# First-chunk head of an attention-plus-feed-forward kernel: v in two halves around W, first h block in halves, first q norms from column sums

## The chip, the cores and the metric

The kernel runs on one core of a Trainium2 chip. The metric is device time in microseconds (us) of one execution; lower is better. Most executions agree within 0.3%.

## The reference

```python
qn = q / (np.linalg.norm(q, axis=1, keepdims=True) + 1e-06)    # q, k, v: 4 x 6144 x 256
kn = k / (np.linalg.norm(k, axis=1, keepdims=True) + 1e-06)
s = kn.transpose(0, 2, 1) @ qn / tau                           # 256 x 256 per batch
a = softmax(s)
x = v @ a
h = np.maximum(np.maximum(x @ w1, x @ w2), x @ w3)             # W: 256 x 768
out = h @ w_out                                                # 768 x 256
```

The kernel folds the softmax matrix into W (called `aw`), so that each chunk of 512 tokens needs `v @ aw`, two maxima and the product with W_out.

## The kernel before

The loads are queued by GpSimd in this order: k and q of the first batch, v's first chunk, W in three column parts of three matrices each, v's second chunk. The DMA queue is the limit of this stretch: its share in the prediction's table of windows is 0.96 up to 21 us and 1.11 up to 34.3 (packets of one engine overlap, so a share can pass 1).

```python
    load_v(0)
    for fp in range(d_ff // FT):
        load_w(fp)                     # three loads each: w1, w2, w3
    load_v(1)
    ...
    ps = gram(0)                       # k squares, then q-by-k and q-by-q products (for q's norms)
    warm_ps = htile("warm_ps")
    for i in range(6):
        PE.matmul(warm_ps, lhsT=ident, rhs=warm, start=(i == 0), stop=(i == 5))
    et = softmax_t(*ps)                # VectorE reduces q-by-q diagonals, then Ln, Exp, Exp
    v_transpose_pe(0)
    aw = alloc_aw()
    rinv = aw_first(et, aw)
    v_transpose(1)                     # DMA transpose of v's second chunk, waits for its load
    ...
    hold_loads(1)                      # GpSimd copies one column of that transpose
    POOL.dma_start(out=wo_sb, in_=moe_w_out.rearrange("(fc p) d -> p fc d", p=P))   # W_out
    load_v(2)
    load_v(3)
```

W_out is issued only after `hold_loads(1)`, a copy that waits until v's second chunk has been loaded and transposed. The first output product comes after eight h blocks (all six of the first chunk and two of the second) and the two later parts of `aw`, and it waits for W_out.

## Time and profile before

| | before |
|---|---|
| median of the runs | 573.48 us (573.35 to 573.7) |
| span of the profiled run | 571.9 us |
| v's second chunk issued / landed | 36.74 / 42.38 us |
| W_out landed, first output product starts | 51.02, 51.07 us |

The profile is read from the end of the head backwards: TensorE has no gap from 51.1 to 560 us, so the question is only when it gets there, and the chain of waits names what it was waiting for. The lines are in the prediction below. One view is not in it: GpSimd's own timeline, here of the kernel before (start, duration, instruction, count, and in brackets the idle time ahead of it with what ended it).

```profile
31.94 2.91 POOL L135 DMA_DIRECT2D w_sb<-in_moe_w_dram  x4 [1.38 <-DMA q_sb<-in_q_dram]
35.34 1.41 POOL L135 DMA_DIRECT2D w_sb<-in_moe_w_dram  x2 [0.49 <-DMA v_sb<-in_v_dram]
36.74 0.59 POOL L110 DMA_DIRECT2D v_sb<-in_v_dram  x1
```

Each issue waits for an earlier load to land; the issue at 35.34 waited for v's first chunk, which landed at 35.06, eight loads earlier in the queue.

### The profile page before, as it was taken

To read this page: it belongs to the slowest core of one execution; us is meant where nothing else is said; L and a number is where in the kernel's file an instruction comes from. 1 tells how busy PE (TensorE), PEld (TensorE's weight loads), DVE (VectorE), ACT (ScalarE), POOL (GpSimd) and SP (SyncE) were. 2 spreads that over 40 slices of the span, in tenths; PEclk is the share of its full clock that TensorE was granted. 3 is DMA by queue.
4 is the path that set the end of the run, shared out by engine and by line. 5 is a ranking of instruction groups with operands and counts; after the bars stand their busy time and mean duration, and the time that the engine had idled before them with its cause. 6 is when DMAs were issued, how large, how long until landed. Compare 5 with 4: busy or idle time off the path is not lost.

```text
span 571.9 us, 9438 instructions
## 1 busy us (share of the span) xinstructions
PE 552.9 (97%) x3344; PEld 329.1 (58%) x3344; DVE 415.9 (73%) x658; ACT 309.1 (54%) x540; POOL 233.3 (41%) x237
## 2 busy tenths in 40 slices
PE   3799999999999999999999999999999999999997
PEld 2665555555755555555575555555575555555566
DVE  0048777777887777777767777777768778778775
ACT  1044567767464576776535467767635444444443
POOL 2442357776460078776560048777750000000000
PEclk9999999999999999999999999999999999999999
DMA  9997999895479268975279339985437333132112
GB/s 143 106 147 121 132 238 138 158 133 107 111 83 171 70 109 157 135 149 107 57 133 149 97 79 141 147 143 99 122 81 160 75 77 108 56 104 64 56 55 76
DMA packets 76960, 65.64 MB, mean 115 GB/s; under 512 B 52464, under 2 KB 62576, under 8 KB 76784
## 3 DMA queue, kind: packets, MB, share of 16 engines
q0 software_dynamic: 19072, 26.48, 39.1%
q1 hardware_dynamic: 57696, 38.41, 24.1%
q8 instruction: 26, 0.43, 0.3%
q14 instruction: 22, 0.18, 0.1%
q10 hardware_dynamic: 144, 0.13, 0.1%
HBM read 78.64 MB, written 25.17 MB: 182 GB/s over the span
## 4 chain that ended last, share of the span: by engine, by line
PE 90%; DMA 6%; issue 2%; POOL 1%; DVE 0%; POOLq 0%
PE h_ps L378 64%; PE o_ps L398 22%; DMA v_sb<-in_v_dram 3%; PE gram L249 3%; PE ew_ps L300 2%; DMA q_sb<-in_q_dram 1%; DMA wo_sb<-in_moe_w_out_dram 1%; DMA vt_sb<-v_sb 1%; POOL k_sb L99 0%; PE o_ps L423 0%; POOL w_sb L135 0%; POOL q_sb L102 0%; DVE o_sb L450 0%; POOL ident masks.py:199 0%; PE rs_ps L288 0%
## 5 line engine op out<-in xcount | busy, mean ns | idle before, releaser
L378 PE MATMUL h_ps<-vt_sb,aw_sb 128*128 128x512 bf16 (+1 forms) x1764 | 406.6, 375 | 0.1
L378 PEld LDWEIGHTS <-aw_sb 128*128 128x128 bf16 x1764 | 171.7, 98 | 161.7 <-DVE aw_sb L306 2.4
L383 DVE TENSOR_TENSOR s_mx<-h_ps,s_mx 128x512 bf16<-128x512 f32 (+1 forms) x294 | 198.8, 676 | 82.2 <-ACT s_mx L382 82.0
L382 ACT ACTIVATE s_mx<-h_ps 128x512 bf16<-128x512 f32 (+1 forms) x294 | 172.3, 586 | 124.3 <-PE h_ps L378 123.4
L384 DVE TENSOR_TENSOR ht_sb<-h_ps,s_mx 128x512 bf16<-128x512 f32 (+1 forms) x294 | 200.2, 681 | 30.6
L208 POOL TENSOR_TENSOR acc<-acc,sq 128x768 f32<-128x768 f32 x88 | 144.3, 1649 | 69.3 <-ACT sq L200 53.1
L398 PE MATMUL o_ps<-wo_sb,ht_sb 128*128 128x256 bf16 x1128 | 153.8, 273 | 0.1
L398 PEld LDWEIGHTS <-ht_sb 128*128 128x128 bf16 x1128 | 110.4, 98 | 52.2 <-issue 0.3
L401 ACT ACTIVATE o_sb<-o_ps 128x512 f32<-128x512 f32 x94 | 56.1, 597 | 83.9 <-PE o_ps L398 83.9
L110 POOL DMA_DIRECT2D v_sb<-in_v_dram x48 | 27.8, 584 | 37.4 <-DMA vt_sb<-v_sb 35.2
L200 ACT ACTIVATE sq<-q_sb 128x768 bf16<-128x768 fp8e4 x48 | 40.5, 844 | 0.0
L200 ACT ACTIVATE sq<-k_sb 128x768 bf16<-128x768 fp8e4 x48 | 40.1, 835 | 0.0
L205 POOL CAST acc<-sq 128x768 f32<-128x768 bf16 x6 | 4.9, 821 | 65.7 <-ACT sq L200 65.7
L102 POOL DMA_DIRECT2D q_sb<-in_q_dram x33 | 18.4, 565 | 4.1 <-DMA v_sb<-in_v_dram 3.1
L168 PE MATMUL kk<-k_sb 128*128 128x256 fp8e4 x48 | 7.5, 338 | 12.3 <-DVE k_sb L154 6.5
L99 POOL DMA_DIRECT2D k_sb<-in_k_dram x29 | 16.1, 557 | 2.9 <-issue 1.1
L249 PE MATMUL gram<-k_sb,q_sb 128*128 128x512 fp8e4 x144 | 16.8, 276 | 0.0
L249 PEld LDWEIGHTS <-q_sb 128*128 128x256 fp8e4 x144 | 15.9, 136 | 0.6
L303 ACT ACTIVATE aw_sb<-ew_ps,rinv 128x384 bf16<-128x384 f32 (+1 forms) x24 | 13.1, 554 | 5.7 <-PE ew_ps L300 4.8
L221 POOL PARTITION_ALL_REDUCE tot<-acc x6 | 10.9, 1858 | 11.9 <-DVE s_mx L383 6.0
L300 PE MATMUL ew_ps<-w_sb,et 128*128 128x384 bf16 (+1 forms) x96 | 15.6, 313 | 0.0
L168 PEld LDWEIGHTS <-k_sb 128*128 128x256 fp8e4 x48 | 6.4, 182 | 13.2 <-DMA k_sb<-in_k_dram 6.7
(64 smaller groups left out, 116.5 us busy)
## 6 DMA issues: line engine op xcount, KB each, us to landing
out_dram<-o_sb SPq DMA_DIRECT2D x41, 512.0 KB, 2.9
v_sb<-in_v_dram POOLq DMA_DIRECT2D x48, 256.0 KB, 4.4
k_sb<-in_k_dram POOLq DMA_DIRECT2D x24, 192.0 KB, 5.9
q_sb<-in_q_dram POOLq DMA_DIRECT2D x24, 192.0 KB, 7.3
out_dram<-o_sb SPq DMA_DIRECT2D x13, 256.0 KB, 2.0
k_sb<-in_k_dram POOLq DMA_DIRECT2D x5, 256.0 KB, 11.2
w_sb<-in_moe_w_dram POOLq DMA_DIRECT2D x9, 128.0 KB, 5.7
kf<-in_k_dram SPq DMA_DIRECT2D x1, 1024.0 KB, 5.0
```

Source lines behind the costliest of these rows:

```text
L102: POOL.dma_start(out=qk[b][0][:, g0:g0 + w, :], in_=q_r[b][:, g0:g0 + w, :])
L110: POOL.dma_start(out=t, in_=v_r[gi // NCH, gi % NCH])
L200: ACT.activation(out=sq, in_=src, func=AF.Square)
L208: POOL.tensor_tensor(out=acc, in0=acc, in1=sq, op=ALU.add)
L249: PE.matmul(g[:, j * C:(j + 1) * C], lhsT=qt[:, tsl, j * P:(j + 1) * P], rhs=kt[:, tsl, :], start=(tp == 0 and j == 0), stop=(tp == NG // ...
L300: PE.matmul(ew[:, :w], lhsT=et[:, j, ic * P:(ic + 1) * P], rhs=w_sb[m][:, j, fsl], start=(j == 0), stop=(j == CC - 1))
L378: PE.matmul(t.rearrange("p (t n) -> p t n", n=P), lhsT=aw[m][:, ic, fsl], rhs=vt[:, tsl, ic, :], start=(ic == 0), stop=(ic == CC - 1))
L382: ACT.activation(out=s_mx, in_=hp[0], func=AF.Copy)
L383: DVE.tensor_tensor(out=s_mx, in0=hp[1], in1=s_mx, op=ALU.max)
L384: DVE.tensor_tensor(out=ht, in0=hp[2], in1=s_mx, op=ALU.max)
L398: PE.matmul(st["ps"][:, half], lhsT=ht[:, fc, t * P:(t + 1) * P], rhs=wo_sb[:, fc, :], start=(fc == 0), stop=(fc == FC - 1))
L401: ACT.activation(out=st["o"][:, t - 1:t + 1, :].rearrange("p t d -> p (t d)"), in_=st["ps"], func=AF.Copy)
```

## The change

Its intent is to start the first h block sooner: q's norms are ready earlier (squares on ScalarE and VectorE while q arrives, summed by one-column products, instead of q-by-q products that VectorE reduces at the end); half of v is loaded and transposed while W's first part comes in; and the first h block is cut in two halves of tokens, so that it can start on the first.

```diff
-    load_v(0)
-    for fp in range(d_ff // FT):
+    POOL.dma_start(out=v_tiles[0][:, 0:HT, :], in_=v_r[0, 0][:, 0:HT, :])
+    load_w(0)
+    POOL.dma_start(out=v_tiles[0][:, HT:TPC, :], in_=v_r[0, 0][:, HT:TPC, :])
+    for fp in range(1, d_ff // FT):
         load_w(fp)
...
-                PE.matmul(ps[j][:, C:C + P], lhsT=qt[:, tsl, jsl], rhs=qt[:, tsl, jsl],
-                          start=False, stop=last, perf_mode=DR, skip_group_check=True)
+        def squares(g0, w):
+            ...
+            ACT.activation(out=a[:, 0:h, :], in_=ra, func=AF.Square)
+            DVE.tensor_tensor(out=d[:, 0:h, :], in0=rd, in1=rd, op=ALU.mult)
+        def columns(rows, first=False, last=False):
+            for n, (t, r) in enumerate(rows):
+                for j in range(CC):
+                    PE.matmul(nq[:, j:j + 1], lhsT=t[:, r, j * P:(j + 1) * P], rhs=ones_c, ...)
...
-    for i in range(6):
-        PE.matmul(warm_ps, lhsT=ident, rhs=warm, start=(i == 0), stop=(i == 5))
-    et = softmax_t(*ps)
-    v_transpose_pe(0)
+    for i in range(2):
+        PE.matmul(warm_ps, lhsT=ident, rhs=warm, start=(i == 0), stop=(i == 1))
+    et = softmax_first(*first)
+    v_transpose_pe(0, 0, HT)
     aw = alloc_aw()
     rinv = aw_first(et, aw)
+    v_transpose_pe(0, HT, TPC)
     v_transpose(1)
...
-                h_block(gi, aw, fc)
+                if gi == 0 and fc == 0:
+                    h_block(gi, aw, fc, slice(0, HT))
+                    h_block(gi, aw, fc, slice(HT, TPC))
+                else:
+                    h_block(gi, aw, fc)
```

The order of products inside `aw_first` changes a little as well, and VectorE alone now copies the transposed v out of PSUM (ScalarE had done half). The guard copy and the load of W_out behind it stay as they were.

More of the change, by code (lines that the diff above doesn't have):

```diff
@@ L75 @@
     sq_pool = ctx.enter_context(tc.tile_pool(name="sq", bufs=4))
+    sqq_pool = ctx.enter_context(tc.tile_pool(name="sqq", bufs=3))
     sm = ctx.enter_context(tc.tile_pool(name="sm", bufs=2))
@@ L118 @@
     SP.dma_start(out=kf, in_=k_r[0][:, 0:HEAD, :])
-    for load, widths in ((load_k, [8] * 5), (load_q, [8] * 4 + [4, 4, 4, 2, 2])):
+    QW = [8] * 4 + [4, 4, 4, 2, 2]
+    for load, widths in ((load_k, [8] * 5), (load_q, QW)):
         g0 = HEAD if load is load_k else 0
@@ L135, in load_w @@
             POOL.dma_start(out=wt[:, :, fsl], in_=w.rearrange("(cc p) f -> p cc f", p=P)[:, :, fsl])
-    load_v(0)
-    for fp in range(d_ff // FT):
+    HT = TPC // 2
+    v_tiles[0] = v_pool.tile([P, TPC, C], BF16, name="v_sb")
+    POOL.dma_start(out=v_tiles[0][:, 0:HT, :], in_=v_r[0, 0][:, 0:HT, :])
+    load_w(0)
+    POOL.dma_start(out=v_tiles[0][:, HT:TPC, :], in_=v_r[0, 0][:, HT:TPC, :])
+    for fp in range(1, d_ff // FT):
         load_w(fp)
@@ L157, with gram_first @@
     neg_ln_tau = -math.log(float(tau)) if float(tau) != 1.0 else 0.0
-    def gram(b):
-        qt, kt = qk[b]
+    def gram_first():
+        qt, kt = qk[0]
         kk = htile("kk")
@@ L173, in gram @@
             DVE.tensor_tensor(out=dkm[:, jsl], in0=kk[:, jsl], in1=ident, op=ALU.mult)
-        ps = [xtile(f"gram{j}") for j in range(CC)]
-        for tp in range(NG // 2):
-            tsl = slice(2 * tp, 2 * tp + 2)
-            last = tp == NG // 2 - 1
-            for j in range(CC):
-                jsl = slice(j * P, (j + 1) * P)
-                PE.matmul(ps[j][:, 0:C], lhsT=qt[:, tsl, jsl], rhs=kt[:, tsl, :],
-                          start=(tp == 0), stop=last, perf_mode=DR, skip_group_check=True)
-                PE.matmul(ps[j][:, C:C + P], lhsT=qt[:, tsl, jsl], rhs=qt[:, tsl, jsl],
-                          start=False, stop=last, perf_mode=DR, skip_group_check=True)
-            if tp == 11:
+        g = xtile("gram")
+        nq = htile("nq")
+        def squares(g0, w):
+            h = w // 2
+            a = sqq_pool.tile([P, QW[0] // 2, C], BF16, name="sqa")
+            d = sqq_pool.tile([P, QW[0] // 2, C], BF16, name="sqd")
+            ra, rd = qt[:, g0:g0 + h, :], qt[:, g0 + h:g0 + w, :]
+            ACT.activation(out=a[:, 0:h, :], in_=ra, func=AF.Square)
+            DVE.tensor_tensor(out=d[:, 0:h, :], in0=rd, in1=rd, op=ALU.mult)
+            return [(t, r) for t in (a, d) for r in range(h)]
+        def columns(rows, first=False, last=False):
+            for n, (t, r) in enumerate(rows):
+                for j in range(CC):
+                    PE.matmul(nq[:, j:j + 1], lhsT=t[:, r, j * P:(j + 1) * P], rhs=ones_c,
+                              start=(first and n == 0 and j == 0), stop=(last and n == len(rows) - 1),
+                              skip_group_check=True)
+        g0 = 0
+        rows = None
+        for i, w in enumerate(QW):
+            if rows:
+                columns(rows, first=(i == 1))
+            for tp in range(g0 // 2, (g0 + w) // 2):
+                tsl = slice(2 * tp, 2 * tp + 2)
+                for j in range(CC):
+                    PE.matmul(g[:, j * C:(j + 1) * C], lhsT=qt[:, tsl, j * P:(j + 1) * P], rhs=kt[:, tsl, :],
+                              start=(tp == 0 and j == 0), stop=(tp == NG // 2 - 1), perf_mode=DR,
+                              skip_group_check=True)
+            rows = squares(g0, w)
+            g0 += w
+            if i == 2:
                 kb_ps = htile("kb_ps")
@@ L190, in gram @@
                 ACT.activation(out=rkb, in_=lnk, func=AF.Exp, scale=-0.5)
-        return ps, rkb
+        columns(rows, last=True)
+        return [g[:, j * C:(j + 1) * C] for j in range(CC)], rkb, nq[:, 0:CC]
     SQW = 3
@@ L265, in exp_t, with softmax_first @@
         return et
-    def softmax_t(ps, rkb):
-        n2q = sm.tile([P, CC], FP32, name="n2q")
-        scr = sm.tile([P, P], FP32, name="scr")
-        for j in range(CC):
-            DVE.tensor_tensor_reduce(out=scr, in0=ps[j][:, C:C + P], in1=ident, scale=1.0, scalar=0.0,
-                                     op0=ALU.mult, op1=ALU.add, accum_out=n2q[:, j:j + 1])
+    def softmax_first(gs, rkb, n2q):
         lnq = sm.tile([P, CC], FP32, name="lnq")
@@ L276, in softmax_t @@
         ACT.activation(out=rq, in_=lnq, func=AF.Exp, scale=-0.5, bias=neg_ln_tau)
-        return exp_t(scaled([ps[j][:, 0:C] for j in range(CC)], rkb), rq)
+        return exp_t(scaled(gs, rkb), rq)
     def alloc_aw():
@@ L325, in products @@
                               start=(j == 0), stop=(j == CC - 1))
+        sums(0)
         products(0, (0, 1))
-        sums(0)
         sums(1)
         DVE.reciprocal(out=rinv, in_=rs_ps[:, 0:CC])
-        products(1, (0, 1))
+        for ms in ((0,), (1,)):
+            products(1, ms)
         for j in range(CC):
@@ L354, in v_transpose, with v_transpose_pe @@
         SP.dma_start_transpose(out=vt_tile(gi), in_=v_sb.rearrange("p t c -> p (t c)"))
-    def v_transpose_pe(gi):
-        v_sb = v_tiles.pop(gi).rearrange("p t c -> p (t c)")
-        vt = vt_tile(gi)
+    def v_transpose_pe(gi, t0, t1):
+        if gi not in vts:
+            vt_tile(gi)
+        v_sb = v_tiles[gi]
         vt_ps = xtile("vt_ps", cols=TPC * C, dtype=BF16)
-        for i in range(TPC * CC):
-            PE.matmul(vt_ps[:, i * P:(i + 1) * P], lhsT=v_sb[:, i * P:(i + 1) * P], rhs=ident,
-                      is_transpose=True, start=(i == 0), stop=(i == CC * TPC - 1))
-        half = TPC * CC // 2
-        ps = vt_ps.rearrange("p (i n) -> p i n", n=P)
-        DVE.tensor_copy(out=vt[:, half:, :], in_=ps[:, half:, :])
-        ACT.activation(out=vt[:, :half, :], in_=ps[:, :half, :], func=AF.Copy)
+        n = (t1 - t0) * C
+        for i in range(n // P):
+            t, cc = t0 + i // CC, i % CC
+            PE.matmul(vt_ps[:, i * P:(i + 1) * P], lhsT=v_sb[:, t, cc * P:(cc + 1) * P], rhs=ident,
+                      is_transpose=True, start=(i == 0), stop=(i == n // P - 1))
+        DVE.tensor_copy(out=vts[gi][:, t0:t1, :, :].rearrange("p t cc n -> p (t cc n)"), in_=vt_ps[:, 0:n])
     def h_block(gi, aw, fc, tsl=slice(0, TPC)):
@@ L417, in last_chunk @@
         dst = out_r[gi // NCH, gi % NCH]
-        HT = TPC // 2
         def products(ps, t0, i, fcs):
@@ L452, in last_chunk @@
         SP.dma_start(out=dst[:, HT + 1, :], in_=o_sb[:, HT + 1, :])
-    ps = gram(0)
+    first = gram_first()
     warm_ps = htile("warm_ps")
-    for i in range(6):
-        PE.matmul(warm_ps, lhsT=ident, rhs=warm, start=(i == 0), stop=(i == 5))
-    et = softmax_t(*ps)
-    v_transpose_pe(0)
+    for i in range(2):
+        PE.matmul(warm_ps, lhsT=ident, rhs=warm, start=(i == 0), stop=(i == 1))
+    et = softmax_first(*first)
+    v_transpose_pe(0, 0, HT)
     aw = alloc_aw()
     rinv = aw_first(et, aw)
+    v_transpose_pe(0, HT, TPC)
     v_transpose(1)
```

## The prediction

> **What bounds the kernel now.** I read the page first, then its timeline part by part. The page says that TensorE is the bound over the whole span, and its strip says where it is not: only in the first two and a half slices of 14.3 us and in the last.
>
> ```profile
> PE 552.9 (97%) x3344; PEld 329.1 (58%) x3344; DVE 415.9 (73%) x658; ACT 309.1 (54%) x540; POOL 233.3 (41%) x237
> PE   3799999999999999999999999999999999999997
> ```
>
> The table of windows (busy us of each engine, count in brackets, granted clock, DMA share, GB/s) puts edges to it. From 51.10 to 560 us TensorE is busy for every 100 ns of it. So nothing that only shifts that stretch can change its length: the time of the kernel is the moment at which TensorE enters it (51.1 us) plus a fixed 520.8 us. The change touches only what is before.
>
> ```profile
> 0.00:21.00 21.00, 7.54 (x49) 6.42 (x49) 1.64 (x7) 2.34 (x2) 7.90 (x19) 1.00 0.96 131
> 21.00:34.30 13.30, 11.48 (x99) 10.48 (x100) 0.01 (x1) 0.80 (x2) 5.46 (x9) 1.00 1.11 119
> 34.30:51.10 16.80, 16.74 (x105) 9.23 (x104) 14.49 (x31) 10.47 (x22) 4.64 (x8) 1.00 0.89 131
> 51.10:300.00 248.90, 248.90 (x1480) 145.22 (x1480) 192.25 (x296) 152.59 (x262) 144.18 (x138) 1.00 0.74 129
> 300.00:560.00 260.00, 260.00 (x1549) 151.07 (x1548) 200.97 (x309) 138.75 (x243) 71.15 (x64) 1.00 0.49 101
> ```
>
> What fixes 51.1? The chain of the first 80 us in order of time (start, us, what) answers with no TensorE work at all before it, only loads:
>
> ```profile
> 16.32 7.09 DMA q_sb<-in_q_dram
> 23.69 11.37 DMA v_sb<-in_v_dram
> 35.34 1.40 POOL w_sb L135 x2
> 36.74 5.64 DMA v_sb<-in_v_dram
> 42.39 2.89 DMA vt_sb<-v_sb
> 45.35 0.18 POOL guard L469
> 45.57 5.45 DMA wo_sb<-in_moe_w_out_dram
> 51.07 0.82 PE o_ps L398 x6
> ```
>
> The load of v's second chunk lands at 42.38, its DMA transpose ends at 45.28, the guard copy waits for that and lets the load of W_out go, and W_out lands at 51.02. The first output product (L398) starts at 51.07. That this was a wait and no coincidence is in TensorE's own timeline:
>
> ```profile
> 34.26 1.47 PE L458 MATMUL warm_ps<-warm,ident 128*128 128x512 bf16 x6
> 35.56 0.61 PE L361 MATMUL vt_ps<-ident,v_sb 128*128 128x128 bf16 x8
> 36.10 0.70 PE L324 MATMUL ew_ps<-w_sb,et 128*128 128x256 bf16 x4
> 36.74 1.03 PE L324 MATMUL ew_ps<-w_sb,et 128*128 128x256 bf16 x8
> 37.73 1.46 PE L378 MATMUL h_ps<-vt_sb,aw_sb 128*128 128x512 bf16 x6
> 44.37 6.63 PE L378 MATMUL h_ps<-vt_sb,aw_sb 128*128 128x512 bf16 x30
> 51.07 0.82 PE L398 MATMUL o_ps<-wo_sb,ht_sb 128*128 128x256 bf16 x6
> 51.72 1.46 PE L378 MATMUL h_ps<-vt_sb,aw_sb 128*128 128x512 bf16 x6
> ```
>
> Six h products take 1.29 us start to start everywhere (51.72 to the next group at 53.01), so 30 take 6.48 and would have let the output product start at 44.37 + 6.48 = 50.85. It starts at 51.07: **TensorE already waits 0.22 us for W_out**, and the table's 0.06 us of missing busy time hides most of it, since the end of the last h product is drawn long.
>
> **What the Trainium skill says.** "DMA: Bandwidth & Descriptors", section "Bandwidth", measures 425 GB/s for large loads of one core and 435 as the ceiling of its 16 engines. The trace agrees: the k-squares groups start at 13.62, 16.11 and 18.54, one load of 1.05 MB (8 x 128 x 256 floats) each 2.45 us, 428 GB/s. So the queue of loads is full from 2 to 41 us, and only bytes move it. "TensorE: Matmul & The Clock Gate", section "What's actually happening", says that the array runs at half clock until a window of some 3.4 us was busy. Agreed: the Gram products of the first q piece step by 0.32 us a pair, and by 0.165 from 24.89 on, 3.9 us after the first. "SBUF — State Buffer", section "SBUF: two separate sides", warns that a VectorE operation in a two-port mode keeps GpSimd from writing descriptors; "VectorE: DVE Perf Modes", section "Why tensor_tensor can't do 2×_2P or 4×", says that the new squares cannot be in such a mode. No run here shows either yet.
>
> **The change part by part.**
>
> *q norms.* Removed: 48 q-by-q products (some 0.06 us each at full clock, in the 0.165 pair) and, behind the last q piece (lands 33.84), two VectorE reductions with their accumulator reads, 34.29 to 35.03. That chain then went on: lnq 35.07, rq 35.30, exp of j=0 35.54 to about 36.0. Added: squares of each piece, half on ScalarE, half on VectorE, and 96 one-column products. A square of 1024 elements should take about 1.1 us (768 take 0.84 in this kernel), inside the 2.45 us of a piece; the four one-column row sums (L318) step by some 27 ns, so 16 columns cost 0.5 us a piece at full clock. After the last piece: square of 256 elements 0.45 (34.3), four columns with their drain 0.3 (34.6), lnq and rq 0.45 (35.1), with the two scalings (0.38 each) beside them on VectorE, done at 35.0. Exp of j=0 is done at 35.6, not 36.0: **0.4 us gained**.
>
> *v and W.* v's halves read 0.26 MB each, the three first W pieces 0.26 MB each, some 0.65 us apiece. Before, v landed at 35.06 and the three W pieces by about 37.0, just when m=2's products came. After: v's first half 34.4, W 35.1, 35.7 and 36.4, v's second half 37.0. So 0.65 us of W's wait is gone, and the second half's four transposes (0.3 us of TensorE, 0.42 of VectorE) are put after W's products.
>
> *Start of h.* Sums and products from 35.6: row sum, four products 36.2, row sums with et of j=1 36.3, eight products 37.2, transposes 37.5. The first h half (six products of 0.108) can then run 37.5 to 38.15, but its m=2 needs W's last eviction at 37.9, and the second half needs the second copy, which VectorE does after its three evictions: 38.3. The h block ends at 38.9 to 39.0, against 39.02 before. **Only 0.0 to 0.3 us is left of the gain on TensorE**; VectorE is done with its maxima 0.5 us sooner, though the split costs it four operations of 0.42 for two of 0.69.
>
> *The wait for W_out.* The bytes ahead of v's second chunk are the same (v0 0.52, W 2.36, itself 0.52 MB). The extra load does not delay its issue: each issue waits for the load eight places before (the ninth q load goes out at 21.23, the first q landed at 21.0; the ninth W-phase wait in the profile is on v), which puts it at about 36.8 against 36.74, some 4 us ahead of its data. So it lands at 42.4, W_out at 51.0 again. TensorE comes to it at 50.6 to 50.85, instead of 50.85, and waits 0.2 to 0.5 us instead of 0.22. **Sum: 0.0 us**, since a minimum of two arrivals is not moved by the earlier one.
>
> **The rivals.**
>
> *The gain goes through.* If W_out came 0.3 to 0.5 us sooner, TensorE's own gain of up to 0.3 plus its wait of 0.22 would count: 573.0. Against it, DMA busy until 41.1 us with the same bytes. For it, only run-to-run luck of completions.
>
> *W_out comes later.* v in 2 KB instead of 4 KB reads, or squares on VectorE that hold up GpSimd's issues. Every 0.1 us there is 0.1 us of the kernel: 573.6 to 574.0. For it, that the chain has no slack at all; against it, GpSimd idles 0.5 to 2 us ahead of most issues of that stretch, and the queue has a reserve.
>
> *A cold array.* One-column products may count less as activity than the q-by-q products that they replace. Cold, a full piece is 8 Gram products of 0.213 and 16 columns of perhaps 0.055: 2.6 us, more than the 2.45 between landings; TensorE would then be late by about 2 us after the last piece, which is more than it waits for W_out: 575. For it, the k squares, busy half the time, never warmed the array; against it, TensorE would still be without a gap from 21 us on.
>
> **Range and chances.** The centre is the old median less a tenth for the first rival, 573.4 us. Run-to-run spread is 0.35 us, a late W_out gives up to 0.5, a cold array (one in ten) 1.5. So 572.8 to 574.2 for eight in ten. Two per cent is 11.5 us, more than all of the head that is touched has to give, so within 2% has 0.98.
>
> **What would show it.** Right: a matmul gap of 0.2 to 0.6 us ahead of the first output product, W_out landing within 0.3 us of 51.02, exp about 0.4 us sooner, the first h block starting 0.1 to 0.4 us sooner. Wrong: W_out landing more than 0.3 us from 51.02, no gap ahead of L398's successor, Gram pieces still at half clock after 26 us, or TensorE gaps after 51 us.

## The result, and the profile after

| | before | after |
|---|---|---|
| median of the runs | 573.48 us (573.35 to 573.7) | 574.99 us (574.96 to 575.33) |
| span of the profiled run | 571.9 us | 573.6 us |

The ratio is 1.0027, with a 95% interval of 1.001 to 1.0045. It is the mean time of the changed kernel's fast runs over that of the other's of the same rounds, so not quite the ratio of the medians. The change costs 1.5 us. The time is outside the predicted range of 572.8 to 574.2. Each profiled run is the slowest of its kernel: 575.33 after (the three others are 574.96 to 575.0) and 573.68 before (the others 573.35 to 573.5), which is to be kept in mind below.

The first line is from the page of the changed kernel: the group of the output products with, last, the idle time ahead of them.

```profile
L425 PE MATMUL o_ps<-wo_sb,ht_sb 128*128 128x256 bf16 x1128 | 153.9, 273 | 0.9 <-DMA wo_sb<-in_moe_w_out_dram 0.9
```

Before, this group's idle time was 0.1 us without a cause. Now 0.9 us is put down to W_out, in one wait. The chain of the first 80 us of the changed kernel (start, us, what) has the same links as before and one more W issue with a wait ahead of it; each link is later from the issue of v's second chunk on.

```profile
23.68 11.13 DMA v_sb<-in_v_dram
...
35.09 0.71 POOL w_sb L137
...
36.08 1.40 POOL w_sb L137 x2
37.48 5.71 DMA v_sb<-in_v_dram
43.20 2.88 DMA vt_sb<-v_sb
46.14 0.19 POOL guard L496
46.37 5.93 DMA wo_sb<-in_moe_w_out_dram
```

v's second chunk is issued at 37.48 (36.74 before) and lands at 43.19 (42.38). Its transpose takes 2.88 us (2.89). W_out's own load takes 5.93 us (5.45) and lands at 52.30 (51.02). So W_out is 1.28 us late: 0.81 from v's second chunk and 0.48 from its own load (the two sum to 1.29; the view rounds). TensorE's timeline of the changed kernel shows its other side.

```profile
35.84 0.38 PE L349 MATMUL ew_ps<-w_sb,et 128*128 128x256 bf16 x2
36.50 0.38 PE L349 MATMUL ew_ps<-w_sb,et 128*128 128x256 bf16 x2 [0.29 <-DMA w_sb<-in_moe_w_dram]
...
38.12 1.57 PE L405 MATMUL h_ps<-vt_sb,aw_sb 128*128 128x256 bf16 x12
...
44.81 6.63 PE L405 MATMUL h_ps<-vt_sb,aw_sb 128*128 128x512 bf16 x30
52.34 0.81 PE L425 MATMUL o_ps<-wo_sb,ht_sb 128*128 128x256 bf16 x6 [0.90 <-DMA wo_sb<-in_moe_w_out_dram]
```

TensorE waits for a W piece until 36.50, starts h at 38.12 instead of 37.73, and by the same reckoning as in the prediction is ready for the first output product at 44.81 + 6.48 = 51.29, where it was ready at 50.85 before. It starts it at 52.34. It waits 1.05 us for W_out, against 0.22 before. So two things are worse: TensorE's own arrival by 0.44 us, hidden behind the second, and W_out's arrival by 1.28 us, which sets the time.

What is left: by the times of the two profiled runs (573.68 and 575.33 us) the kernel grew by 1.65 us, the start of the output products by 1.27. The other 0.38 us arises later. The chain of waits around the switch to the second batch shows 0.33 of it in two groups of products; these are the lines before and then after.

```profile
168.28 1.95 PE ew_ps L300 x12
170.23 1.48 PE h_ps L378 x6
```

```profile
169.60 2.11 PE ew_ps L325 x12
171.71 1.65 PE h_ps L405 x6
```

The profiled execution is 0.33 to 0.37 us slower than the three others of the changed kernel, so this piece may belong to that execution alone; there is no profile of another, and why these groups were slower is not known.

**Where the delay of v's second chunk arises.** GpSimd's timeline of the changed kernel answers to the one shown of before.

```profile
32.65 2.10 POOL L137 DMA_DIRECT2D w_sb<-in_moe_w_dram  x3 [0.64 <-DMA q_sb<-in_q_dram]
35.09 0.71 POOL L137 DMA_DIRECT2D w_sb<-in_moe_w_dram  x1 [0.34 <-DMA v_sb<-in_v_dram]
36.08 1.40 POOL L137 DMA_DIRECT2D w_sb<-in_moe_w_dram  x2 [0.28 <-DMA w_sb<-in_moe_w_dram]
37.48 0.55 POOL L111 DMA_DIRECT2D v_sb<-in_v_dram  x1
```

The issue at 35.09 waited for v's first half, which landed at 34.81; the one at 36.08 for the first W piece, which landed at 35.79. The landings, from the trace's own records (the views round the time to landing to 0.1):

| landed (us) | before | after |
|---|---|---|
| last q piece | 33.83 | 33.72 |
| v's first half, then the first W piece | (v whole 35.06) | 34.81, then 35.79 |
| v whole and three W pieces | 37.05 | 37.84 |
| all of W | 41.13 | 41.86 |
| v's second chunk | 42.38 | 43.19 |

At the last q piece the changed kernel is 0.11 us ahead. When v and three W pieces have landed, it is 0.8 us behind, and it stays so: the rest takes 5.3 us in both. From one landing to the next, v's first half takes 1.09 us and the first W piece 0.98, where the later half takes 0.70 and later W pieces 0.64 to 0.73. The windows of 1 us (busy us of each engine with counts, clock, DMA share, and last the GB/s written) show the same stretch from the queue's side, before and then after.

```profile
32.00:33.00 1.00, 1.00 (x14) 0.92 (x12) 0.00 (x0) 0.00 (x0) 0.90 (x2) 1.00 1.21 174
33.00:34.00 1.00, 0.85 (x10) 0.68 (x9) 0.00 (x0) 0.00 (x0) 1.00 (x2) 1.00 1.19 190
34.00:35.00 1.00, 1.00 (x8) 0.64 (x9) 0.57 (x5) 0.00 (x0) 0.85 (x2) 1.00 1.41 192
```

```profile
32.00:33.00 1.00, 1.00 (x15) 0.73 (x13) 0.52 (x1) 0.53 (x1) 0.36 (x2) 1.00 1.24 157
33.00:34.00 1.00, 0.91 (x17) 0.77 (x16) 0.71 (x3) 0.69 (x3) 1.00 (x2) 1.00 1.34 172
34.00:35.00 1.00, 0.90 (x11) 0.36 (x10) 0.96 (x3) 0.62 (x3) 0.75 (x2) 1.00 1.39 181
35.00:36.00 1.00, 0.62 (x9) 0.37 (x7) 0.49 (x2) 0.91 (x2) 0.71 (x1) 1.00 1.33 192
```

Between 32 and 35 us the changed kernel writes 157, 172 and 181 GB/s where it was 174, 190 and 192: 46 KB less, about 0.24 us at the 192 GB/s that follow. Two things change in this stretch: v moves in 2 KB reads, and from 32 to 34 us ScalarE and VectorE are busy with squares (0.52 to 0.71 us of each) where they had idled.

Not every DMA engine is behind, though. The records of single packets have the first packet of v's first chunk start at 32.00 us before and 32.03 after, and the first of its second chunk at 39.47 and 39.43: the earliest engine is level throughout. The last packet of the second chunk starts at 41.93 and 42.68, 0.75 us later: it is the engines that come last that lost the time. (The records don't name the engine.)

### The profile page after: what moved, and what is told of

The parts are those of the page before. It is cut to its first block, busy times and chain, and to the rows that moved or that the text cites. A ratio compares the mean times of both kernels' runs of the same rounds, so it can differ in the third digit from the quotient of the medians.

```text
span 573.6 us, 9569 instructions
## 1 busy us (share of the span) xinstructions
PE 554.4 (97%) x3394; PEld 330.0 (58%) x3394; DVE 423.8 (74%) x666; ACT 315.7 (55%) x549; POOL 234.3 (41%) x238
## 4 chain that ended last, share of the span: by engine, by line
PE 90%; DMA 6%; issue 2%; POOL 1%; DVE 0%; POOLq 0%
PE h_ps L405 63%; PE o_ps L425 22%; DMA v_sb<-in_v_dram 3%; PE gram L279 3%; PE ew_ps L325 2%; DMA q_sb<-in_q_dram 1%; DMA wo_sb<-in_moe_w_out_dram 1%; DMA vt_sb<-v_sb 1%; POOL k_sb L100 0%; PE o_ps L449 0%; POOL w_sb L137 0%; POOL q_sb L103 0%; DVE ht_sb L411 0%; DVE o_sb L476 0%; POOL ident masks.py:199 0%
## 5 line engine op out<-in xcount | busy, mean ns | idle before, releaser
L111 POOL DMA_DIRECT2D v_sb<-in_v_dram x47 | 27.3, 585 | 36.8 <-DMA vt_sb<-v_sb 35.3
L189 ACT ACTIVATE sqa<-q_sb 128x1024 bf16<-128x1024 fp8e4 (+2 forms) x9 | 6.8, 769 | 18.2 <-DMA q_sb<-in_q_dram 17.6
```

The source lines that it names most:

```text
L111: POOL.dma_start(out=t, in_=v_r[gi // NCH, gi % NCH])
```

## The experiments

None ran to a result. Four explanations of the 0.8 us were in play. A: the changed kernel needs 100 more TensorE instructions (50 products, each with a weight load), and these come as 16 KB packets over the same DMA engines, so a packet that used to fall where the queue of loads is empty (44.86 us) now falls where it is full (38.99 us). B: the two half loads of v cost the queue more than one whole. C: with one load more ahead of it, v's second chunk is issued 0.74 us later, too late to keep the queue full. D: the squares, which now run while v and W move, slow those loads.

**Undoing the norms.** In a stand-in for the changed kernel the old Gram function and softmax come back; v's halves stay.

```diff
-    first = gram_first()
+    first = gram(0)
-    for i in range(2):
+    for i in range(6):
-    et = softmax_first(*first)
+    et = softmax_t(*first)
```

> A stand-in for the changed kernel, since the chip takes no matmul performance mode at present: each DoubleRow product, which takes two rows of tokens at once, is one ordinary product over the first of the two rows; number, order and shapes of instructions stay, the result is wrong on purpose. In it the q norms are as before (q-by-q products, reductions on VectorE, six warm-up products); v's halves, W's place between them and the halves of the first h block are kept. Theory D (the squares, or what comes with them, slow the loads behind q): v's first half lands at about 34.5, the first W piece at 35.1, v's second chunk at 42.4 to 42.6, time 573.5 to 574.0. Theory B (the half loads cost it): first W piece at 35.8, v's second chunk at 43.2, time 574.6 to 575.2.

Measured: nothing, no chip ran it.

**Undoing the half loads.** In the same stand-in, v's first chunk is loaded whole; the norms stay.

```diff
-    POOL.dma_start(out=v_tiles[0][:, 0:HT, :], in_=v_r[0, 0][:, 0:HT, :])
+    POOL.dma_start(out=v_tiles[0], in_=v_r[0, 0])
     load_w(0)
-    POOL.dma_start(out=v_tiles[0][:, HT:TPC, :], in_=v_r[0, 0][:, HT:TPC, :])
```

> The same kind of stand-in for the changed kernel (each DoubleRow product an ordinary one over one row; wrong on purpose), with v's first chunk loaded whole ahead of W; the norms with their squares and all TensorE instructions stay as changed. Theory D: v lands at 35.5 or later and the first W piece 0.65 after it, v's second chunk at 42.9 to 43.2, time 574.4 to 575.1. Theory B: v lands at 35.06, its second chunk at 42.4 as before, time 573.5 to 573.9.

Measured: nothing, no chip ran it.

**Moving the instruction packet alone.** The kernel before with 48 one-column products of zeros between its k squares. For this explanation the traces themselves speak against it: the second packet of the changed kernel starts at 38.99 us, while the delay is complete by 37.8 us, before it, and does not grow after it by more than 0.1 us (0.79 at 37.84, 0.74 at 41.86, 0.81 at the landing of v's second chunk). The view of the DMA queues from 38 to 43 us shows the packet in the changed kernel (queue, kind: packets, MB, share); the same view of the kernel before has no such line.

```profile
q0 software_dynamic: 962, 0.65, 91.2%
q8 instruction: 1, 0.02, 1.2%
```

So A is not needed for the delay, which is an argument from order in time and not an experiment. C fares no better: v's second chunk was issued 0.74 us later, and yet its first packet started at 39.43 us, where it had started at 39.47.

**Freeing W_out.** The load of W_out issued ahead of the guard copy, in the changed kernel. It would have shown how much of the 1.5 us is the wait for W_out, and it is the version that might beat both kernels when joined with an earlier W. It is untried:

> The changed kernel with the load of W_out issued ahead of the guard copy, so that it follows v's second chunk in the queue and no longer waits for its transpose. If the wait for W_out is the whole of what TensorE waits for at its first output product (0.90 us of idle time there, plus what the end of the last h product hides: 44.81 + 6.48 = 51.29 against 52.34, so 1.05), W_out lands before 47 us and the time falls by 1.05 to 573.9 (573.6 to 574.2), which is still not below the kernel before, since TensorE itself comes 0.44 us later than the 50.85 of before. If the wait is replaced by one for the second chunk's transpose, the time stays at 575.

## Why the prediction was wrong

**The bound: right, but for 0.4 us.** The table of windows has TensorE busy for 247.66 of the 247.70 us from 52.3 to 300 and for all 260.00 up to 560 (the stretched products at the switch of batches do not show there, since ends of products are modelled), and the wait for W_out ahead of the first output product is there and has grown. The stretch from that product on, which the prediction held fixed at 520.8 us, took 521.2 in the profiled execution. The mechanism, that the later of two arrivals sets the time, holds: TensorE at 51.29, W_out at 52.30, start at 52.34. (The prediction writes "a minimum of two arrivals"; it means the later one, and its sum uses it so.)

**The q norms: right.** Exp starts at 35.03 instead of 35.54, 0.51 us sooner, for the 0.4 predicted. The rival of a cold array was half right. These lines are from TensorE's timeline of the changed kernel:

```profile
23.44 1.97 PE L208 MATMUL gram<-k_sb,q_sb 128*128 128x512 fp8e4 x8
25.21 0.42 PE L196 MATMUL nq<-ones_c,sqa 128*128 128x1 bf16 x8
...
25.88 1.97 PE L208 MATMUL gram<-k_sb,q_sb 128*128 128x512 fp8e4 x8
...
30.99 0.63 PE L208 MATMUL gram<-k_sb,q_sb 128*128 128x512 fp8e4 x4
```

Eight Gram products take 1.77 us to the next group at 23.44 and still 1.76 at 25.88, 0.22 us each, and four take 0.47 at 30.99, 0.12 each. So the array stepped at half speed past 26 us, which the prediction named as a sign that it would be wrong, where before it stepped at full speed from 24.89. TensorE was busy for 10.85 of the 11 us from 21 to 32 us (9.33 before), and still it came to full speed later; this suggests that the one-column products count for less as activity, but no run tested it. But a piece at half speed fits between two landings (the groups start 2.44 us apart), and TensorE caught up: it finishes with q at 34.55, 0.8 us behind the last landing. The rival's 2 us of lateness did not come.

**v and W: wrong, and this is the step that failed.** The prediction took "some 0.65 us apiece" from bytes alone, and had the first half land at 34.4 and the W pieces at 35.1, 35.7 and 36.4. They landed at 34.81, 35.79, 36.46 and 37.14. The term of v's first half and the first W piece, 1.3 us together, measured 2.07 (33.72 to 35.79): "only bytes move it" did not hold. What follows is the 0.7 us by which the first W piece was then late:

- W's second matrix is waited for until 36.50, so the h block starts 0.39 us later instead of up to 0.3 sooner.
- The step "the extra load does not delay its issue" gave 36.8 us. The rule that it used, that each issue waits for the load eight before, fits: the two issues that slipped waited for the first half and for the first W piece. With those late, the issue came at 37.48. This slip cost nothing by itself, since the chunk's first packet started no later than before (39.43 us, 39.47 before).
- v's second chunk landed at 43.19 instead of 42.4. The step "the bytes ahead are the same" was true of the bytes and not of the time they took.

**W_out's own load: not foreseen.** It took 5.93 us instead of 5.45. It starts in an empty queue in both kernels, and its first packets took up to 1.17 us in the changed kernel's trace, up to 0.81 before. Why is open, and one execution of each does not tell whether it repeats.

**The rivals.** "W_out comes later" is what happened; it was given up to 0.5 us and took 1.28. Of its two reasons, squares that hold up GpSimd's issues are not seen: the nine W issues took 0.70 to 0.73 us each in both kernels. The other, 2 KB reads, is taken up below. The range was at fault too: the text itself said that the chain has no slack and that every 0.1 us there is 0.1 us of the kernel, and then gave the loads no more than half a microsecond.

**What stays open.** Why the two loads behind q took 1.09 and 0.98 us. The trace bounds one part: a packet with a 4 KB read takes 172 ns in this stretch and one with a 2 KB read 97, so v's 128 reads of 4 KB sum to 8 x 172 = 1376 ns on each of 16 engines and its 256 of 2 KB to 16 x 97 = 1552, 0.18 us more. This is an estimate, since packets of one engine overlap; the landings say the same (v whole took 1.23 us, two halves at the pace of the second, 0.70, would take 1.40). So B can be some 0.2 us of the 0.8, and it should slow every engine alike, while the earliest engine lost nothing. The rest was lost by the engines that come last: between 32.8 and 35.0 us the changed kernel's packet records have eighteen stretched ones of 116 to 525 ns, where their like take 60 (1 KB read) or 98 (2 KB), and by the same count the kernel before has none in that time. That these packets are what delayed the last engines is an inference. They lie beside the squares, and also beside GpSimd's issues; but the issues ran there before as well (31.94 to 34.85 us) and stretched nothing. Nor is a square enough by itself: squares also ran from 29.5 to 32.0 us, with no stretched packet from 28.9 to 32.8, and the kernel before, without squares, has a few stretched ones near 28 and 31 us. So neither B nor D is shown, and no run was to be had to tell them apart.

**The Trainium skill beside the traces.** "DMA: Bandwidth & Descriptors", section "Why a DMA increments its semaphore by 16 and not by 1", has a DMA run on up to 16 engines that finish independently, and complete only when all have posted. The traces agree: the loads that land from 28 to 43 us end in 16 packets of 4 bytes each (272 for 17 loads before, 288 for 18 after), and v's second chunk landed 0.81 us late though its first packet was not late at all. It is this that the prediction left out. "Runtime: NRT & Kernel Launch", section "Instruction fetch mechanics", says that instructions come in 16 KB blocks of 256 by a DMA queue of the sequencer's own, mostly hidden; the packets of 16 KB are there, 0.96 us (38.99 us, after) and 1.22 us (44.86 us, before) on one engine, and no wait of TensorE in the head is put down to one.

## What to carry to other kernels

Find the link that sets the end of a head before improving another: here W_out waited behind a guard, with no slack, and work saved on TensorE could not have shown. A change that reorders loads is not neutral because the bytes are: a load lands with its slowest engine, and while the queue stays full, every later load lands as late. Where issues wait for landings eight places back, look as well whether a late issue empties the queue; here it did not. When a chain has no slack, let the range be as wide as the loads in it can slip.

## What the Trainium skill lacked or had wrong

- "DMA: Bandwidth & Descriptors" has measured rates by the size of a whole load, but no time of a packet by the size of its read. For loads that cast float to bfloat16, the trace has 172 ns for a packet with a 4 KB read, 97 for 2 KB and 60 for 1 KB, which is what a change of the piece size needs.
- No page has the limit seen in both traces: a GpSimd issue waited for the landing of the load eight places before it (issue at 35.34 after the landing at 35.06, before; at 35.09 after 34.81, in the changed kernel).
- No page has that single packets are long at the start of a load into an empty queue (W_out: up to 0.81 us before, 1.17 after, against 0.06 later in the same load).
